# Batch 1's first transform: twelve columns by sums and differences, and a new order in the first block

## The chip, the cores and the metric

The kernel runs on one core of a Trainium2 chip. Its time is the device time of one execution in microseconds; runs of the kernel before took 863.89, 864.54 and 865.01 (median 864.54). One more execution was profiled. Engines are named as the profile names them: PE (TensorE; PEld is its weight load), DVE (VectorE), ACT (ScalarE), POOL (GpSimd) and SP (SyncE, which only issues DMAs here).

## The reference

Two stages follow each other. `x` is 8 batches of 3008 tokens by 256 features in fp32. First, each feature is filtered along the tokens with a real FFT; then a gated feed-forward net runs over all 24064 tokens.

```
X = np.fft.rfft(x, axis=1)
y = np.fft.irfft(X * (filt_r + 1j * filt_i)[None], n=3008, axis=1)
gate = np.maximum(y @ w_gate, 0.0)      # 256 -> 1536
val = y @ w_val                         # 256 -> 1536
out = (gate * val) @ w_out              # 1536 -> 256
```

## The kernel before

**The transform.** The 3008 tokens are seen as 94 rows (n1) by 32 columns (n2). A first product over n1 (the "A" stage) gives 48 frequencies k1, real and imaginary part, for each column. A turn brings columns onto partitions; `fwd` is the product over n2, `product` multiplies with the filter's real part (`tt`, k = 0) and imaginary part (`uu`, k = 1), `inv` goes back over n2, a second turn follows, and `item_c` goes back over n1 and leaves `yT`. `gv` then makes one 128-wide piece of gate and value for 512 tokens: two matmuls into psV, two into psG, a copy of psV by ACT (`vsb`), and one DVE instruction for `prod`. `o_part` multiplies prods with `w_out`.

**Order.** Nothing is scheduled by the framework: each engine runs its instructions in the order of the text. The first block's work is written out by hand: batch 0's A stage, `first_b` (batch 0 from `fwd` to `inv`, with batch 1's A stage put between as `item`s), `turn_d`, the first `item_c`s, and then 47 blocks of 12 `gv`s. Later batches' stages hang on step numbers in `side`. For batches 2 to 7 the A stage works with folded rows: POOL forms sums and differences (`fold_chunk`), and `tiled_a` runs sixteen fp32 matmuls of 24 rows by 32 columns on sixteen tiles of PE. Batches 0 and 1 use one full fp32 matmul for 512 columns instead (`a_bank`).

**Batch 1's A stage** is 16 items: (p, s, h) is columns 8p + 4s to 8p + 4s + 3 and half h of the features. An item is a matmul in `a_bank` and one or two ACT copies (`a_1`). The first half of the features goes to `AS1[0]`, inside dCb, and through DRAM (`store_half`, `load_half`); the rest goes to two `asb` tiles that DVE turns in `turn_1`. Its x comes in 12 DMAs on SP (`load_x`), each to every fourth of 128 partitions, in the order of the columns, behind a small DMA (`hold`) that waits for filter data.

**PSUM banks.** `bank` takes the bank that was given back longest ago (`free.pop(0)`), `done` puts one back. So the order of `done` calls in the text says which earlier reader an instruction waits for.

**Memory.** The prologue's tiles (pool `pro`) hold WA, tabs (with conj and M1's source), the products of batch 0 and more. `prologue.close()` at line 696 frees them, and pool `fs` (vsb, prod, osb and others) takes the same memory.

**POOL's list in this part** is: the six products of `ON_POOL` (it reads a copy `xs` that ACT makes of PSUM), `place_own`, the loads of WvT, WgT (two halves each) and WoT (two halves), the copy of M1, the sign change of Fti (line 694, which reads conj), and later the loads of batch 2's x.

Of the kernel before, what the change touches and what calls it, by code (L numbers as in the profile page):

```python
# [12 lines left out]
FP32 = mybir.dt.float32  # L13
BF16 = mybir.dt.bfloat16
ALU = mybir.AluOpType
# [14 lines left out]
N1, N2 = 94, 32  # L30
# [86 lines left out]
def kernel(  # L117
# [20 lines left out]
    assert NB * W == B * S  # L138

    wa_h, fold_h, f2_h, tab_h = _tables()  # L140

    ctx.enter_context(tc.manual_schedule())
    consts = ctx.enter_context(tc.tile_pool(name="consts", bufs=1))
# [12 lines left out]
    def done(t):  # L156
        free.append(held.pop(id(t))[0])
# [7 lines left out]
    XF = [consts.tile([128, NX2 * D], FP32, name=f"XF{c}") for c in range(N2 // NX2)]  # L165
    XP = [t[:, i * 2048:i * 2048 + 2048].rearrange("p (k d) -> p k d", d=512) for t in XF for i in range(2)]
    WA = pro.tile([128, 128], FP32)
    AS0 = pro.tile([128, 4, N2 // 2, D // 8, 4], BF16)
    DS0 = AS0.rearrange("p q n c f -> p (q n c f)").rearrange("p (k c f) -> p k c f", c=D // 2, f=4)
    dCb = consts.tile([128, 48, D], BF16)  # L170
# [91 lines left out]
    def a_bank(n2, nn, d0, nd):  # L262

        psA = bank("psA", nn, nd)
        xf = XF[n2 // NX2].rearrange("p (n d) -> p n d", d=D)
        n = n2 % NX2
        nc.tensor.matmul(psA, WA, xf[:, n:n + nn, d0:d0 + nd], start=True, stop=True)  # L267
        return psA
# [10 lines left out]
            nc.scalar.copy(dst[:, :, q.start + i], src[:, :, i])  # L279
        done(psA)  # L280

    def a_1(p, s, h):

        psA = a_bank(NC2 * p + 4 * s, 4, h * D // 2, D // 2)
        if h and len(AS1) == 1:
            for _ in range(2):
                t = sb.tile([128, NC2 * D], BF16, tag="asb", bufs=3, name="asb")
                AS1.append(t.rearrange("p (l c d) -> p l c d", l=NC2, c=N2 // NC2))
        ts = AS1[1:] if h else AS1[:1]
        w = D // 2 // len(ts)  # L290
        for i, t in enumerate(ts):
            nc.scalar.copy(t[:, 4 * s:4 * s + 4, p, :], psA[:, :, i * w:(i + 1) * w])
        done(psA)

    def turn_a(dst, src):

# [17 lines left out]
    def new_at(b):  # L314
        shape = [2, 32, D // 2] if b else [16, D // 2, 4]
        ats[b] = sb.tile([128, *shape], BF16, tag="at", bufs=1, name="at")
# [70 lines left out]
            nc.sync.dma_start(ats[b][:, 8 * z:8 * z + 8].rearrange("p j d -> p (j d)"),  # L387
                              _ap(Abuf[b], 8 * z * D, [[NG * D, 128], [1, 8 * D]]))

    ON_POOL = ((0, 1), (1, 1), (2, 1))  # L390
    ats = {}

    psXs, tus, left, xs = {}, {}, {}, {}
# [43 lines left out]
    def inv(b, q):  # L437

        psD = [bank("psD", 2, D) for c in range(4)]
        last = 0 if b else 1  # L440
        for m in range(2):
            for k in range(last + 1):
                for r in range(2):
                    for c in range(4):
                        for e in range(2):
                            i = 2 * q + m
                            nc.tensor.matmul(psD[c][64 * e:64 * e + 64, m],  # L447
                                             (I2t, I2u)[k][32 * c:32 * c + 32, r, 2 * i + e, :],
                                             tus[b, i, e, k][32 * c:32 * c + 32, r],
                                             start=(k == r == 0), stop=(k == last and r == 1),  # L450
                                             tile_position=(32 * c, 64 * e))
        dst = sb.tile([128, 8, D], BF16, tag="dsb", bufs=3, name="dsb") if b else DS0
        def out(cs):
            for c in cs:
                copy = nc.vector.tensor_copy if (c % 2 if b else (q, c) in ((1, 3), (2, 0), (2, 1))) else nc.scalar.copy
                if b:
                    copy(dst[:, c:8:4, :], psD[c])
                else:
                    k, g = 4 * q + c // 2, c % 2 * 2
                    copy(dst[:, k:k + 3:2, :, g:g + 2], psD[c].rearrange("p m (f e) -> p m e f", f=2))  # L460
                done(psD[c])
        if not b:
            return out(range(4))

        def rest():
            out((2, 3))
            for z in range(4):
                nc.sync.dma_start(_ap(Dbuf[b], (64 * (z // 2) + z % 2) * NG * D + 8 * q * D,
                                      [[2 * NG * D, 32], [1, 8 * D]]),
                                  dst[32 * z:32 * z + 32])  # L470
        out((0, 1))
        return rest

    def first_b(item):

        def products(i, es=(1, 0)):
            for e in es:
                for k in range(2):
                    product(0, i, e, k, pool=(i, e) in ON_POOL)

        for i in range(3):
            fwd(0, i)
            if i < 2:
                products(i)
        make_back_u()
        products(2)
        warm(3)
        fwd(0, 3)
        products(3, (1,))
        warm(3)  # L490
        fwd(0, 4)
        item(2)
        products(3, (0,))
        inv(0, 0)
        fwd(0, 5)
        products(4)
        item(2)
        products(5)
        place_own()
        inv(0, 1)  # L500
        item(2)
        inv(0, 2)

    dCs = {}
# [161 lines left out]
            warm(4)  # L666
    hold = sb.tile([2, 8], BF16, tag="hold", bufs=1)
    nc.sync.dma_start(hold, Ftr[0:2, 4, 0:8])
    load_x(1, sp, ((0, 0, 2 * q), (0, 2 * q, 4 * q), (1, 0, 2 * q), (1, 2 * q, 4 * q)))
    items = iter([(p, s, h) for p in range(4) for h in range(2) for s in range(2)])  # L670

    def item(n):
        for _ in range(n):
            p, s, h = next(items)
            a_1(p, s, h)
            if (p, s, h) == (3, 1, 0):
                new_at(1)
                store_half(1)
                load_half(1)

    first_b(item)
    load_vg(0, DFF // 2)
    load_vg(DFF // 2, DFF)
    load_o()
    nc.gpsimd.tensor_copy(M1, tabs[:, 578:].rearrange("p (l n) -> p l n", l=2))
    for h in range(2):
        turn_d(h)
    item(7)
    for m in range(y_items(0)):
        for h in range(2):  # L690
            item_c(m, h)
    item(3)
    turn_1(0)
    nc.gpsimd.tensor_scalar(Fti, Fti, conj[:, 0:1], 1.0, op0=ALU.mult, op1=ALU.mult)
    nc.sync.dma_start(WF, nc.inline_tensor(fold_h, name="dft_fold").ap())
# [89 lines left out]
```

## Time and profile before

| | us |
|---|---|
| median of three runs | 864.54 |
| profiled execution | 863.39 |
| its span | 861.6 |
| PE busy | 853.8 |
| DVE busy | 578.6 |
| ACT busy | 500.2 |
| POOL busy | 458.0 |
| start of the first psX (batch 0's fwd) | 22.33 |
| start of the first psV | 45.85 |
| start of the first psO | 57.49 |

In a timeline a line gives the start and the duration in us, the engine, the source line, the operation, what it writes and reads, its shape and the number of merged instructions; in brackets stands the idle time ahead of it and what ended it. In a table of windows each engine's busy time comes with its number of instructions, followed by PE's granted clock, the DMA engines' mean busy share and GB/s. Matmuls are pipelined, so a duration is longer than the distance to the next start.

### The profile page before, as it was taken

The page shows a single profiled execution, that of the slowest core. Times are in us where ns is not written, and L with a number is a line of the kernel's source. Part 1 is how long each engine was busy: PE and PEld are TensorE (multiplying, and loading weights), DVE is VectorE, ACT ScalarE, POOL GpSimd, SP SyncE. Part 2 cuts the span into 40 slices and gives each one's busy share as a digit, 9 for nine tenths or more (in the row PEclk, how much of TensorE's full clock was granted, in tenths as well). Part 3 has the DMA queues.
Part 4 walks back from the last instruction along what each step waited for, and adds up shares of the span by engine and source line. Part 5 has one row for each costly group of instructions (what it writes and reads, how often), then busy time and mean ns, then how long its engine had stood idle before and what let it go on. Part 6 is the DMA issues. An engine that isn't in the chain of part 4 may idle for free.

```text
span 861.6 us, 20366 instructions
## 1 busy us (share of the span) xinstructions
PE 853.8 (99%) x7614; PEld 497.3 (58%) x7614; DVE 578.6 (67%) x864; ACT 500.2 (58%) x944; POOL 458.0 (53%) x494
## 2 busy tenths in 40 slices
PE   9999999999999999999999999999999999999997
PEld 4456655656556555665556665565655656666665
DVE  3878865777657876577765787658766578555554
ACT  5765565556655565555655565655565555565552
POOL 6747890488986765776667756867550033000001
PEclk9999999999999999999999999999999999999999
DMA  9995375333762339534294333842454222511112
GB/s 248 239 166 124 98 156 145 104 113 106 195 190 79 80 92 190 175 84 102 73 211 153 99 101 94 201 147 77 103 118 119 97 62 51 129 39 31 37 32 55
DMA packets 102862, 101.60 MB, mean 118 GB/s; under 512 B 21703, under 2 KB 89959, under 8 KB 101995
## 3 DMA queue, kind: packets, MB, share of 16 engines
q1 hardware_dynamic: 83407, 77.93, 34.1%
q0 software_dynamic: 18848, 21.68, 11.6%
q8 instruction: 60, 0.98, 0.5%
q10 hardware_dynamic: 508, 0.68, 0.3%
q14 instruction: 39, 0.32, 0.1%
HBM read 58.23 MB, written 45.88 MB: 121 GB/s over the span
## 4 chain that ended last, share of the span: by engine, by line
PE 98%; DMA 1%; SPq 1%; issue 0%; ACT 0%; DVE 0%
PE psV L578 29%; PE psO L599 29%; PE psG L578 28%; PE psF L369 3%; PE psA L267 3%; PE psY L561 3%; PE psD L447 2%; PE psX L404 1%; DMA XF<-in_x_dram 1%; SPq L192 1%; PE psI L209 0%; ACT AS L460 0%; DVE XF L608 0%; SPq L637 0%
## 5 line engine op out<-in xcount | busy, mean ns | idle before, releaser
L583 DVE SCALAR_TENSOR_TENSOR prod<-psG,vsb 128x512 bf16<-128x512 f32 x564 | 389.5, 691 | 234.0 <-ACT vsb L581 229.9
L581 ACT CAST vsb<-psV 128x512 bf16<-128x512 f32 x564 | 332.4, 589 | 217.6 <-PE psV L578 210.2
L599 PE MATMUL psO<-WoT,prod 128*128 128x256 bf16 x2256 | 336.5, 273 | 0.0
L578 PE MATMUL psV<-yT,WvT 128*128 128x512 bf16 x1128 | 336.2, 380 | 0.0
L578 PE MATMUL psG<-yT,WgT 128*128 128x512 bf16 x1128 | 335.3, 379 | 0.0
L599 PEld LDWEIGHTS <-prod 128*128 128x128 bf16 x2256 | 220.7, 98 | 143.4
L578 PEld LDWEIGHTS <-WgT 128*128 128x128 bf16 x1128 | 110.0, 97 | 133.9 <-issue 1.1
L434 POOL TENSOR_TENSOR pp<-tt,uu 128x256 bf16<-128x256 f32 x84 | 61.1, 727 | 169.8 <-DVE uu L424 159.9
L578 PEld LDWEIGHTS <-WvT 128*128 128x128 bf16 x1128 | 100.4, 98 | 36.9 <-issue 25.6
L569 ACT CAST yT<-psY 128x470 bf16<-128x470 f32 (+16 forms) x134 | 58.8, 457 | 46.6 <-PE psY L561 46.5
L608 ACT COPY osb<-psO 128x512 f32<-128x512 f32 x92 | 53.9, 586 | 25.2 <-PE psO L599 24.1
L621 POOL DMA_DIRECT2D out_dram<-osb x5 | 2.6, 539 | 119.2 <-ACT osb L608 117.7
L424 DVE TENSOR_TENSOR tt<-psX,Ftr 128x512 f32<-128x512 f32 (+1 forms) x93 | 63.5, 683 | 0.5 <-PE psX L404 0.5
L424 DVE TENSOR_TENSOR uu<-psX,Fti 128x512 f32<-128x512 f32 (+1 forms) x93 | 63.3, 681 | 0.2 <-DMA Fti<-in_filt_i_dram 0.2
L435 POOL TENSOR_TENSOR pp<-tt,uu 128x256 bf16<-128x256 f32 x84 | 61.0, 726 | 0.0
L355 POOL TENSOR_TENSOR fold<-XF 128x1024 f32<-128x1024 f32 x24 | 56.5, 2352 | 4.8 <-DMA XF<-in_x_dram 4.3
L356 POOL TENSOR_TENSOR XF<-XF 128x1024 f32<-128x1024 f32 x24 | 56.5, 2355 | 1.9
L259 POOL CAST scr<-prod 128x8 f32<-128x8 bf16 x19 | 3.6, 192 | 85.7 <-DVE prod L583 85.7
L342 POOL DMA_DIRECT2D XF<-in_x_dram x76 | 45.7, 604 | 2.1 <-issue 1.0
L376 DVE CAST asb<-psF 128x512 bf16<-128x512 f32 x48 | 30.9, 686 | 17.7 <-PE psF L369 17.7
L376 ACT CAST asb<-psF 128x512 bf16<-128x512 f32 x48 | 25.8, 589 | 28.9 <-PE psF L369 28.9
L561 PE MATMUL psY<-M,dCb 96*128 96x94 bf16 (+2 forms) x514 | 39.9, 205 | 0.0
(68 smaller groups left out, 456.4 us busy)
## 6 DMA issues: line engine op xcount, KB each, us to landing
Dbuf<-dsb SPq DMA_DIRECT2D x84, 128.0 KB
dCb<-Dbuf SPq DMA_DIRECT2D x56, 192.0 KB
XF<-in_x_dram POOLq DMA_DIRECT2D x38, 256.0 KB, 7.4
Abuf<-asb SPq DMA_DIRECT2D x96, 96.0 KB
at<-Abuf SPq DMA_DIRECT2D x18, 512.0 KB
XF<-in_x_dram SPq DMA_DIRECT2D x31, 256.0 KB
XF<-in_x_dram POOLq DMA_DIRECT2D x76, 96.0 KB, 5.2
out_dram<-osb SPq DMA_DIRECT2D x69, 94.0 KB
```

The costliest lines, as they stand in the source:

```text
L355: tt(t, xp[:, 0:2], xp[:, 2:4], op=ALU.add)
L356: tt(xp[:, 2:4], xp[:, 0:2], xp[:, 2:4], op=ALU.subtract)
L376: copy(asf[:, :, q, :], banks[q])
L424: nc.vector.tensor_tensor(p, psX, filt, op=ALU.mult)
L434: nc.gpsimd.tensor_tensor(p[:, 0], tt[:, 0], uu[:, 1], op=ALU.subtract)
L435: nc.gpsimd.tensor_tensor(p[:, 1], tt[:, 1], uu[:, 0], op=ALU.add)
L561: nc.tensor.matmul(psY[:, o:o + w], d_rows(b, col, h), M1[:, 1, n1:n1 + w] if b == 0 else M1[:NROW, 0, n1:n1 + w], start=True, stop=True)
L569: copy(yT[:, h, p:p + w], psY[:, o:o + w])
L578: nc.tensor.matmul(pt[:, :W], w[:, h, ft * 128:(ft + 1) * 128], yT[:, h, y0:y0 + W], start=(h == 0), stop=(h == 1))
L581: nc.scalar.copy(vsb, psV[:, :W])
L583: nc.vector.scalar_tensor_tensor(prod, in0=psG[:, :W], scalar=0.0, in1=vsb, op0=ALU.max, op1=ALU.mult)
L599: nc.tensor.matmul(psO[:, t % 2], prods[ft][:, t * 128:(t + 1) * 128], WoT[:, ft, :], start=(ft == 0), stop=(ft == NFT - 1))
```

## The change

`WH` holds the rows of WA's table for n1 = 0 to 46, once at partitions 0 and once at 64. Since row n1 + 47 has the same coefficient as row n1 up to a sign that is + for even k1 and - for odd ones, sums of the two rows give the even frequencies and differences the odd ones.

- `load_halves` loads nn columns so that partition n1 has rows n1 and n1 + 47 side by side, the first half of the columns at partitions 0 to 47 and the second at 64 to 111. `fold_halves` makes sums and differences on POOL. `a_halves` runs four fp32 matmuls of 47 rows by 64 columns on four tiles, into two banks, and `out_1` copies a bank to the places that `a_1` filled.
- Columns 8 to 15 (two `a_halves`, one for each half of the features) and 28 to 31 (one, with all features) go that way; items are left for p = 0, p = 2 and the first half of p = 3: ten.
- `first_b` has five items, one fewer ahead of `inv(0, 2)`. Its first products are ordered otherwise: on POOL tt, tt, uu, uu of two groups and later the third, on DVE three tt and then three uu. One more copy of `inv(0, 1)` goes to DVE.
- On POOL, `fold_halves(8, 8)`, M1 and `fold_halves(28, 4)` stand between the first and the second half of the weights WvT and WgT. On SP, 14 DMAs replace 12.
- `store_half` and `load_half` follow the last `a_halves`, behind the `item_c`s.

```diff
+    wh_h = np.zeros_like(wa_h)
+    n1 = np.arange(N1 // 2)
+    for r in (0, 64):
+        wh_h[r + n1] = wa_h[n1 % 32 * 4 + n1 // 32]
...
+    WH = pro.tile([128, 128], FP32)
...
-    def a_1(p, s, h):
-
-        psA = a_bank(NC2 * p + 4 * s, 4, h * D // 2, D // 2)
-        if h and len(AS1) == 1:
+    def out_1(psA, n2, n, d0, nd):
+
+        if len(AS1) == 1:
...
-        ts = AS1[1:] if h else AS1[:1]
-        w = D // 2 // len(ts)
-        for i, t in enumerate(ts):
-            nc.scalar.copy(t[:, 4 * s:4 * s + 4, p, :], psA[:, :, i * w:(i + 1) * w])
+        l, p = n2 % NC2, n2 // NC2
+        for t, lo, w in zip(AS1, (0, D // 2, 3 * D // 4), (D // 2, D // 4, D // 4)):
+            if d0 <= lo < d0 + nd:
+                nc.scalar.copy(t[:, l:l + n, p, :], psA[:, :, lo - d0:lo - d0 + w])
         done(psA)
+
+    def a_1(p, s, h):
+
+        n2, d0 = NC2 * p + 4 * s, h * D // 2
+        out_1(a_bank(n2, 4, d0, D // 2), n2, 4, d0, D // 2)
+
+    def halves(n2, nn):
+
+        o = n2 % NX2 * D
+        return XF[n2 // NX2][:, o:o + nn * D].rearrange("p (k n d) -> p k n d", k=2, d=D)
+
+    def load_halves(b, n2, nn):
+
+        w = nn // 2
+        for s in range(2):
+            nc.sync.dma_start(halves(n2, nn)[64 * s:64 * s + 48].rearrange("p k n d -> p k (n d)"),
+                              _ap(x, (b * N1 * N2 + n2 + w * s) * D,
+                                  [[N2 * D, 48], [N1 // 2 * N2 * D, 2], [1, w * D]]))
+
+    sums = {}
+
+    def fold_halves(n2, nn):
+
+        xh = halves(n2, nn)
+        sums[n2] = pro.tile([128, nn // 2, D], FP32, tag=f"sum{nn}", name="sum")
+        nc.gpsimd.tensor_tensor(sums[n2], xh[:, 0], xh[:, 1], op=ALU.add)
+        nc.gpsimd.tensor_tensor(xh[:, 1], xh[:, 0], xh[:, 1], op=ALU.subtract)
+
+    def a_halves(n2, nn, d0, nd):
+
+        w, d = nn // 2, slice(d0, d0 + nd)
+        banks = [bank("psA", w, nd) for _ in range(2)]
+        for e, src in ((1, sums[n2]), (0, halves(n2, nn)[:, 1])):
+            for s in range(2):
+                r = 64 * s
+                nc.tensor.matmul(banks[s][64 * e:64 * e + 64], WH[r:r + N1 // 2, 64 * e:64 * e + 64],
+                                 src[r:r + N1 // 2, :, d], start=True, stop=True, tile_position=(r, 64 * e))
+        for s in range(2):
+            out_1(banks[s], n2 + w * s, w, d0, nd)
...
-                copy = nc.vector.tensor_copy if (c % 2 if b else (q, c) in ((1, 3), (2, 0), (2, 1))) else nc.scalar.copy
+                copy = nc.vector.tensor_copy if (c % 2 if b else (q, c) in ((1, 2), (1, 3), (2, 0), (2, 1))) else nc.scalar.copy
...
         for i in range(3):
             fwd(0, i)
-            if i < 2:
-                products(i)
+        for k in range(2):
+            for i in range(2):
+                product(0, i, 1, k, pool=True)
+        for i in range(3):
+            product(0, i, 0, 0)
         make_back_u()
-        products(2)
+        for k in range(2):
+            product(0, 2, 1, k, pool=True)
+        for i in range(3):
+            product(0, i, 0, 1)
...
-        item(2)
+        item(1)
         inv(0, 2)
...
-    load_x(1, sp, ((0, 0, 2 * q), (0, 2 * q, 4 * q), (1, 0, 2 * q), (1, 2 * q, 4 * q)))
-    items = iter([(p, s, h) for p in range(4) for h in range(2) for s in range(2)])
+    load_x(1, sp, ((0, 0, 2 * q),))
+    load_halves(1, 8, 8)
+    nc.sync.dma_start(WH, nc.inline_tensor(wh_h, name="dft_wh").ap())
+    load_x(1, sp, ((1, 0, 2 * q), (1, 2 * q, 3 * q)))
+    load_halves(1, 28, 4)
+    items = iter([(p, s, h) for p in (0, 2, 3) for h in range(2) for s in range(2 - p // 3)])
...
-            if (p, s, h) == (3, 1, 0):
-                new_at(1)
-                store_half(1)
-                load_half(1)
...
     load_vg(0, DFF // 2)
+    fold_halves(8, 8)
+    nc.gpsimd.tensor_copy(M1, tabs[:, 578:].rearrange("p (l n) -> p l n", l=2))
+    fold_halves(28, 4)
     load_vg(DFF // 2, DFF)
     load_o()
-    nc.gpsimd.tensor_copy(M1, tabs[:, 578:].rearrange("p (l n) -> p l n", l=2))
     for h in range(2):
         turn_d(h)
-    item(7)
+    item(3)
+    for h in range(2):
+        a_halves(8, 8, h * D // 2, D // 2)
+    item(2)
     for m in range(y_items(0)):
         for h in range(2):
             item_c(m, h)
-    item(3)
+    a_halves(28, 4, 0, D)
+    new_at(1)
+    store_half(1)
+    load_half(1)
     turn_1(0)
```

More of the change, by code (lines that the diff above doesn't have):

```diff
@@ L388, in load_at_tiled @@
                               _ap(Abuf[b], 8 * z * D, [[NG * D, 128], [1, 8 * D]]))
-    ON_POOL = ((0, 1), (1, 1), (2, 1))
     ats = {}
@@ L478, in products @@
                 for k in range(2):
-                    product(0, i, e, k, pool=(i, e) in ON_POOL)
+                    product(0, i, e, k)
         for i in range(3):
             fwd(0, i)
-            if i < 2:
-                products(i)
+        for k in range(2):
[3 more added lines that the diff above has]
+            product(0, i, 0, 0)
         make_back_u()
-        products(2)
+        for k in range(2):
+            product(0, 2, 1, k, pool=True)
+        for i in range(3):
+            product(0, i, 0, 1)
         warm(3)
@@ L668 @@
     nc.sync.dma_start(hold, Ftr[0:2, 4, 0:8])
-    load_x(1, sp, ((0, 0, 2 * q), (0, 2 * q, 4 * q), (1, 0, 2 * q), (1, 2 * q, 4 * q)))
-    items = iter([(p, s, h) for p in range(4) for h in range(2) for s in range(2)])
+    load_x(1, sp, ((0, 0, 2 * q),))
[4 more added lines that the diff above has]
+    items = iter([(p, s, h) for p in (0, 2, 3) for h in range(2) for s in range(2 - p // 3)])
     def item(n):
         for _ in range(n):
-            p, s, h = next(items)
-            a_1(p, s, h)
-            if (p, s, h) == (3, 1, 0):
-                new_at(1)
-                store_half(1)
-                load_half(1)
+            a_1(*next(items))
     first_b(item)
     load_vg(0, DFF // 2)
+    fold_halves(8, 8)
+    nc.gpsimd.tensor_copy(M1, tabs[:, 578:].rearrange("p (l n) -> p l n", l=2))
+    fold_halves(28, 4)
     load_vg(DFF // 2, DFF)
     load_o()
-    nc.gpsimd.tensor_copy(M1, tabs[:, 578:].rearrange("p (l n) -> p l n", l=2))
     for h in range(2):
         turn_d(h)
-    item(7)
+    item(3)
+    for h in range(2):
+        a_halves(8, 8, h * D // 2, D // 2)
+    item(2)
     for m in range(y_items(0)):
```

## The prediction

> **What bounds the kernel now.** I read the page's chain first, then the waits of TensorE after the prologue (there are none after 57 us), then the timelines of TensorE, POOL, ACT and DVE between 20 and 55 us. Below are two lines of the page and seven of TensorE's timeline (start, duration).
>
> ```profile
> PE   853.8 (99%) x7614; PEld 497.3 (58%) x7614; DVE 578.6 (67%) x864; ACT 500.2 (58%) x944; POOL 458.0 (53%) x494
> ...
> PE 98%; DMA 1%; SPq 1%; issue 0%; ACT 0%; DVE 0%
> ...
> 26.93 1.96 PE L267 MATMUL psA<-XF,WA 128*128 128x512 f32 x4 [0.68 <-DMA XF<-in_x_dram]
> ...
> 35.39 0.42 PE L447 MATMUL psD<-tt,I2t 32*64 32x256 bf16 x16
> ...
> 36.40 6.28 PE L267 MATMUL psA<-XF,WA 128*128 128x512 f32 x14
> 42.66 0.70 PE L561 MATMUL psY<-M,dCb 128*128 128x94 bf16 x12
> 43.20 2.81 PE L267 MATMUL psA<-XF,WA 128*128 128x512 f32 x6
> 45.85 0.59 PE L578 MATMUL psV<-yT,WvT 128*128 128x512 bf16 x2
> ...
> 111.61 1.14 PE L369 MATMUL psF<-XF,WF 24*32 24x512 f32 x32
> ```
>
> TensorE never stops from the first psV (45.85) to the end, so whatever moves the first block's matmuls moves the end by as much. The change works ahead of 45.85. There an item (one fp32 matmul, two records) costs 6.28/7, about 0.86 to 0.9 us. The psF line is sixteen fp32 calls on sixteen small tiles in 1.08 us (111.61 to the next psV at 112.69): two passes of 0.43 and 0.22 for going in and out.
>
> Three other engines meet TensorE there; these are their timelines:
>
> ```profile
> 36.38 2.82 POOL L694 TENSOR_SCALAR Fti<-Fti,tabs 128x3072 bf16<-128x3072 bf16 x1
> ...
> 37.89 4.72 DVE L302 STREAM_TRANSPOSE dCb<-AS 128x2048 f32<-128x2048 f32 x2
> ...
> 46.61 1.32 ACT L581 CAST vsb<-psV 128x512 bf16<-128x512 f32 x2
> ...
> 46.45 1.09 DVE L297 STREAM_TRANSPOSE at<-asb 128x512 f32<-128x512 f32 x1 [2.32 <-ACT asb L292]
> 47.44 1.24 DVE L583 SCALAR_TENSOR_TENSOR prod<-psG,vsb 128x512 bf16<-128x512 f32 x2
> 48.60 1.08 DVE L297 STREAM_TRANSPOSE at<-asb 128x512 f32<-128x512 f32 x1
> 49.58 1.84 DVE L583 SCALAR_TENSOR_TENSOR prod<-psG,vsb 128x512 bf16<-128x512 f32 x3
> ```
>
> POOL is done with the prologue at 39.20 and idle to 53. The first vsb copy writes memory of the closed pool pro, and among its waits is POOL's count at L694, the last use of that pool; today that is 7 us old. DVE runs behind TensorE in the first gv steps: the third prod ends at 50.23.
>
> **The change on TensorE's path.** *Products.* DVE no longer waits 0.2 us for Fti; its 18 products end at 33.66, not 33.96. Nothing waits for that, so it is worth 0. But banks are handed out in the order they were given back. With the new order fwd(0,4) gets the bank of (2,1), which ACT empties into xs from 26.12 to 26.68. fwd(0,4) starts at 26.75, not 25.82, and the item behind it, which waited for its load until 26.93, starts at 27.08 (16 matmuls and the switch are 0.33, from 36.07 to 36.40): 0.15 lost. POOL's six products only change places.
>
> *Last inverse sooner.* One item fewer ahead of it: 35.39 + 0.15 - 0.86 = 34.68. Its operands are ready at 33.66. DVE takes two copies of inverse 1 and two of inverse 2; as in the trace the latter start 1.10 after the inverse, so the transposes start 0.7 sooner and end at 41.9.
>
> *Tiled columns.* inv(0,2) takes 1.01 (35.69); then five items (4.31), two a_halves and the switches. For two in a row I take four passes and one 0.22, 1.95, from the psF row; a third alone 1.08. That gives psY at 42.15, with the transposes hidden (41.9). If nothing overlapped between the four tiles, an a_halves would be 4 x 0.86 = 3.45; psF, the nearest row, says otherwise. psY 0.54, the third a_halves 1.08: first psV at 43.8, where yT, on DVE 1.47 after psY's start as now, is ready at 43.6. TensorE alone gains 2.05.
>
> *Loads on SP.* Fourteen DMAs for twelve, with the same bytes and 64 KB for WH. The two first halves loads put 786 KB on 48 neighbouring partitions each, not on every fourth. Rows of the table of windows:
>
> ```profile
> 28.00:30.00 2.00, 2.00 (x83) 1.00 (x81) 2.00 (x4) 1.26 (x3) 2.00 (x3) 1.00 0.86 328
> 30.00:32.00 2.00, 1.69 (x20) 0.68 (x4) 2.00 (x4) 2.00 (x5) 1.94 (x4) 1.00 1.02 402
> ...
> 46.00:48.00 2.00, 2.00 (x11) 0.88 (x9) 1.55 (x2) 1.74 (x4) 0.00 (x0) 1.00 0.82 164
> 48.00:50.00 2.00, 2.00 (x11) 0.93 (x10) 2.00 (x4) 1.24 (x3) 0.00 (x0) 1.00 0.68 191
> ```
>
> (The last column is GB/s.) Strided loads run at 254 to 402, the store from 24 neighbouring partitions at 164 to 191. 786 KB is 2.0 to 3.1 us or 4.1 to 4.8 us; I take 2 us more, as the store is nearest in shape. The ninth load landed at 31.76; the item ahead of inv(0,2) would get it at 33.8 where it wants it at 33.6: 0.2 at most, covered below. The halves land near 31.2, and those of 28 to 31 near 36.5. [...]
>
> **The change on POOL, which I think decides.** Today, after place_own: two weight DMAs to 32.93, then the rest. Now the folds come in: 2 x 2.35 (as L355/L356, same shape) to 37.65, M1 0.34, two of 128x512 at 1.27 to 40.5. The other four weight DMAs take 3.08 as now (43.6), Fti 2.82: end at 46.5 instead of 39.2. The sums are ready 0.7 before the first a_halves (38.4), those of 28 to 31 two us before theirs. But the first vsb waits for 46.5. ACT would be ready for it at 45.1: the third a_halves leaves it six small copies, 1.2 us by an estimate from its 0.65 for two of 256 columns, and cover for them is gone with POOL's wait anyway. So vsb starts at 46.55, practically when it does now (46.61), and DVE follows it: first prod at 47.2 (now 47.44, where a transpose held it), second 47.8, turn_1(1) 48.4, third 49.4 to 50.05. There are eight banks. The fifth psG needs the first prod's, the seventh psV (now at 51.24) the third prod's, since a psY takes one bank between. So the seventh psV cannot start before 50.1: 1.15 sooner, not 2.05. After that DVE gains 0.26 a step and TensorE is not held again: prod 4 is done at 51.25, wanted at 51.6. The gain is the smaller of the two, 1.15; I round down to 1.1 for waits that POOL takes between DMAs. Up to 0.9 of lateness in TensorE's own part (the loads, the tiles, the 0.15) is hidden by this.
>
> *Weights.* These lines are from the answers for the two tiles. The second halves of WvT and WgT are issued at 40.55 and 41.25, not 32.93 and 33.64, and are wanted at 50.1 and 50.5.
>
> ```profile
> L247 POOL DMA_DIRECT2D WvT<-in_moe_w_val_dram x2: 716/754/793, 31.4 to 32.9; - x2
> ...
> DMA to landing us min/median/max: 6.7/8.6/10.6
> ...
> L247 POOL DMA_DIRECT2D WgT<-in_moe_w_gate_dram x2: 716/722/728, 32.2 to 33.6; - x2
> ...
> DMA to landing us min/median/max: 7.8/9.5/11.2
> ```
>
> The short ones are the first pair, behind x; the long ones queued behind the first pair. With 6.7 and 7.8 they land at 47.3 and 49.1: no stall. With 10.6 and 11.2, at 51.2 and 52.5: 2.0 lost. I take the short ones, as the first pair is long gone by then. The store of batch 1's half (issued near 44.8, now 44.94) meets them, though. WoT, wanted at 56.4, and fwd(1,0), wanted at 59.5 with its half landing at 56.5 now, have 2 to 3 us each.
>
> **Sum.** The profiled execution took 863.39 (span 861.6 and 1.8 around it); the median of the three runs is 864.54, 1.15 above. 864.54 - 1.1 = 863.4. About 0.2% (1.73 us) is what a measurement of this kernel can tell from no change, so my forecast lies inside that.
>
> **Rivals.**
> 1. *The whole gain arrives.* If vsb need not wait for L694, or POOL is done by 45, TensorE's 2.05 stands: 862.5, faster by 0.24%. For it: no stall of this kind is in the trace of before. Against: the order of the wait and POOL's four durations, all from rows. 0.2.
> 2. *The second weights come late* (the slower side). The seventh gv needs WgT's second half; each us after 50.5 costs one, from 51.6 the kernel is slower than before, from 53.4 by more than 0.2%. With the long landings 864.54 - 1.1 + 2.0 = 865.4; if the store (4.1 to 4.8 us at its rate) goes first, WgT lands at 49.1 + 4.5 = 53.6 and the time is 866.5. For it: DMA share is over 1 from 34 to 46 now. Against: the short landings. 0.14.
> 3. *Four tiles don't overlap as sixteen do.* If only second passes queue (1.3 more for each of three), psV starts at 47.7 and the time is 866.4; psF speaks against it. 0.06.
> 4. *The halves land after 32.93*, so POOL's string starts late. It takes 1.7 us more than I count; with 1.1 more there is no gain: 864.5. 0.06.
> My forecast has 0.54.
>
> **How the numbers follow.** Faster: rival 1 and a bit of a TensorE tail, 0.21. Slower: about half of rival 2, rival 3 and 0.02 for what I don't see, 0.15. The rest, 0.64, is within 0.2%. The range goes from rival 1 with the runs' own spread (0.4), 862.1, to rivals 2 and 3 at their middle, 866.2.
>
> **What would show it.** Right: L694 ends near 46.5 and the first vsb starts just behind it; the first psV is near 43.8, the seventh near 50.1, with idle time of TensorE ahead of the fifth psG and the seventh psV put down to DVE prod; an a_halves pair takes about 1.95; fwd(0,4) waits for ACT xs. Wrong: vsb ahead of L694's end, or TensorE idle at the seventh gv put down to a DMA, or 3 us for an a_halves.

## The result, and the profile after

The changed kernel took 869.5 us in the median of 22 runs (866.08 to 871.6), the kernel before 864.11 in 22 runs on the same chip: a ratio of 1.0054 with a 95% interval of 1.0045 to 1.0064. It is slower by half a per cent, where I had forecast 863.4 and at most 866.2. The profiled execution took 870.49 (span 868.7, against 861.6 before: 7.1 more). Ratios and intervals leave out slow runs (more than 1.5% above the fastest of their kernel), which are three of the ten of the kernel without the gate of Fti below, its profiled one among them, while its median is that of all ten.

PE's busy time and the chain that ended last, from the page of the changed kernel:

```profile
PE 854.0 (98%) x7626; PEld 496.7 (57%) x7626; DVE 578.1 (67%) x865; ACT 499.4 (57%) x946; POOL 465.2 (54%) x498
...
PE 93%; DMA 5%; ACT 1%; SPq 1%; issue 0%; DVE 0%; ACTq 0%
```

PE is as busy as before (853.8), so its idle time is 7 us longer, and DMAs have gone from 1% of the chain to 5%. (Busy time hides two terms that cancel here: what the tiles save, and the 1.7 us that a lower clock costs further down.) PE's four longest waits from 20 to 72 us (line and tile, what it waited for, us, times, longest) say where:

```profile
PE psX L446 <- DMA at<-Abuf: 3.7, 1, 3.7
PE psV L626 <- ACT vsb L629: 1.9, 1, 1.9
PE psX L446 <- ACT xs L463: 0.9, 1, 0.9
PE psV L626 <- DVE prod L631: 0.5, 1, 0.5
```

The largest is not one I had priced: `fwd(1,0)` waits for the half of batch 1 that goes through DRAM. The chain in order of time (start, us, what) shows how it got there, and PE's timeline what happened behind it:

```profile
45.75 0.88 SPq L369
...
46.67 6.75 DMA Abuf<-dCb
...
53.48 0.92 SPq L375
...
54.49 11.40 DMA at<-Abuf
...
66.02 0.63 PE psX L446 x31
```

```profile
66.02 0.63 PE L446 MATMUL psX<-at,F 64*32 64x256 bf16 x31 [3.73 <-DMA at<-Abuf]
66.58 0.82 PE L626 MATMUL psV<-yT,WvT 128*128 128x512 bf16 x2
67.19 1.06 PE L626 MATMUL psG<-yT,WgT 128*128 128x512 bf16 x2
68.05 1.06 PE L647 MATMUL psO<-WoT,prod 128*128 128x256 bf16 x4
68.90 1.06 PE L626 MATMUL psV<-yT,WvT 128*128 128x512 bf16 x2
```

Line 369 is `store_half`, line 375 `load_half`. Their issues on SP, in the kernel before (lines 326 and 332) and then in the changed one:

```profile
44.94 2.69 SPq L326 DMA_DIRECT2D Abuf<-dCb  x4
49.60 2.40 SPq L332 DMA_DIRECT2D at<-Abuf  x4
```

```profile
45.39 2.24 SPq L369 DMA_DIRECT2D Abuf<-dCb  x4
52.03 5.71 SPq L375 DMA_DIRECT2D at<-Abuf  x4
```

The last part of the load took 11.4 us from its issue to its landing (5.1 before, by the same semaphore events), and a pair of psG matmuls that took 0.59 us up to 61 takes 1.06 behind the wait: the table of windows gives a granted clock of 0.71 from 66 to 68, 0.50 from 68 to 70 and 0.94 from 70 to 72.

Counting in starts of `vsb` (564 in each kernel, the same work), the changed kernel is behind the kernel before by

| up to `gv` | behind by, us | what came in |
|---|---|---|
| 6 | 1.39 | the gate of the first vsb, less what PE gained ahead of it |
| 14 | 1.39 | |
| 18 | 7.08 | the wait of 4.0 at `fwd(1,0)`, and 1.7 at the reduced clock |
| 200 | 7.08 | |
| 210 | 7.61 | a wait of ACT on Abuf at 353 us |
| 563 | 7.61 | |

and the end comes 0.5 us sooner behind the last vsb, which leaves the 7.1. So nothing goes wrong after 72 us but that one half microsecond.

### The profile page after: what moved, and what is told of

The parts are those of the page before. It is cut to its first block, busy times and chain, and to the rows that moved or that the text cites. A ratio compares the mean times of both kernels' runs of the same rounds, so it can differ in the third digit from the quotient of the medians.

```text
span 868.7 us, 20400 instructions
## 1 busy us (share of the span) xinstructions
PE 854.0 (98%) x7626; PEld 496.7 (57%) x7626; DVE 578.1 (67%) x865; ACT 499.4 (57%) x946; POOL 465.2 (54%) x498
## 4 chain that ended last, share of the span: by engine, by line
PE 93%; DMA 5%; ACT 1%; SPq 1%; issue 0%; DVE 0%; ACTq 0%
PE psO L647 28%; PE psV L626 27%; PE psG L626 27%; PE psY L609 3%; PE psF L412 3%; PE psA L272 2%; PE psD L489 2%; DMA Abuf<-asb 1%; PE psX L446 1%; DMA at<-Abuf 1%; DMA dCb<-Dbuf 1%; DMA Abuf<-dCb 1%; DMA XF<-in_x_dram 1%; SPq L197 0%; PE psA L333 0%; ACT I2u L225 0%
## 5 line engine op out<-in xcount | busy, mean ns | idle before, releaser
L398 POOL TENSOR_TENSOR fold<-XF 128x1024 f32<-128x1024 f32 x24 | 56.4, 2351 | 7.2 <-DMA XF<-in_x_dram 6.7
L399 POOL TENSOR_TENSOR XF<-XF 128x1024 f32<-128x1024 f32 x24 | 56.5, 2354 | 1.9
L385 POOL DMA_DIRECT2D XF<-in_x_dram x76 | 45.6, 602 | 4.6 <-DMA XF<-in_x_dram 2.1
```

What stands on the lines that cost most here:

```text
L398: tt(t, xp[:, 0:2], xp[:, 2:4], op=ALU.add)
L399: tt(xp[:, 2:4], xp[:, 0:2], xp[:, 2:4], op=ALU.subtract)
```

## The experiments

Each kernel ran beside the kernel before on the same chip. This table is worked out from the profiled executions: first psV less first psX is PE's way through the first block, "held" is the time from the store's first issue to its first packet, "load" the time from `load_half`'s first issue to its last landing, and the wait is PE's at `fwd(1,0)` for Abuf.

| kernel | median us | ratio to before, interval | psV - psX | held | load | wait |
|---|---|---|---|---|---|---|
| before | 863.9 to 865.5 | 1 | 23.5 | 0.8 | 6.9 | 0 |
| after | 869.5 | 1.0054, 1.0045 to 1.0064 | 21.7 | 5.0 | 13.9 | 3.7 |
| gate of Fti gone | 872.81 | 1.0058, 1.0022 to 1.0095 | 22.8 | 4.3 | 21.6 | 13.2 |
| weights first | 864.34 | 1.0006, 0.9990 to 1.0022 | 23.8 | 0.8 | 8.5 | 0 |
| 28 to 31 sooner | 866.82 | 1.0025, 1.0008 to 1.0043 | 22.9 | 3.6 | 10.6 | 2.4 |
| before, late weights (first try) | 869.66 | 1.0065, 1.0047 to 1.0083 | 29.5 | 3.7 | 7.1 | 0 |
| before, late weights | 875.33 | 1.0132, 1.0096 to 1.0168 | 23.1 | 4.5 | 15.6 | 4.7 |
| after, batch 2's x later | 874.25 | 1.0103, 1.0084 to 1.0122 | 23.9 | 3.4 | 9.8 | 0.3 |
| before, new products | 865.13 | 1.0011, 0.9991 to 1.0032 | 26.1 | 0.8 | 7.4 | 0 |
| early, old products | 862.59 | 0.9980, 0.9967 to 0.9993 | 23.4 | 0.8 | 8.4 | 0 |
| early, new products | 862.26 | 0.9975, 0.9962 to 0.9988 | 23.8 | 0.8 | 7.6 | 0 |
| split sums | 862.66 | 0.9977, 0.9964 to 0.9989 | 23.6 | 0.8 | 8.9 | 0 |
| split sums, old products | 862.81 | 0.9970, 0.9951 to 0.9990 | 24.6 | 0.8 | 8.5 | 0 |
| split sums, more warm | 862.36 | 0.9961, 0.9948 to 0.9974 | 22.9 | 0.9 | 7.9 | 0 |

### Is it the gate of Fti?

The changed kernel, with Fti's sign taken from a tile of the pool that stays, so that vsb's memory has no reader on POOL any more.

```diff
-    conj32 = pro.tile([128, 2], FP32, tag="conj32", bufs=1)
+    conj32 = consts.tile([128, 2], FP32, name="conj32")
...
-    nc.gpsimd.tensor_scalar(Fti, Fti, conj[:, 0:1], 1.0, op0=ALU.mult, op1=ALU.mult)
+    nc.gpsimd.tensor_scalar(Fti, Fti, conj32[:, 0:1], 1.0, op0=ALU.mult, op1=ALU.mult)
```

> The changed kernel with conj32 kept outside the prologue's pool, so that the sign change of Fti is no longer a last use of that pool. Theory 1 (two waits in a row: first the vsb copies behind Fti, then fwd(1,0) behind batch 1's half, which the second weights hold up in the DMA queues): the first vsb starts near 45.7 instead of 49.1, the seventh psV near 50 to 51 instead of 52.6, but the half lands when it did (65 to 66), so fwd(1,0) only waits longer (5 to 6 us instead of 3.7) and the time stays within 1 us of the changed kernel's. Rival (the vsb wait is what costs the time): 2 to 3 us faster than the changed kernel, 866.5 to 867.5.

The gate is gone: the first vsb starts at 46.1 and not at 49.1, and `gv` 6 is 1.06 us ahead of the kernel before, not 1.39 behind. The time is no better: PE comes sooner to a half that is not there sooner. The ten runs lie between 864.4 and 879.8, wider than those of the changed kernel, and their median is 3.3 above its median, not within 1. The profiled execution is one of the longest three (878.14) and doesn't stand for the median: its half landed at 73.8 and PE waited 13.2 us for it, where I had expected 65 to 66 and 5 to 6. Why its load ran for 21.6 us no run here shows. The gate was real, but a larger wait stood behind it.

### Is it the late weights?

POOL issues the second weights and WoT ten microseconds later than before; its timeline in the kernel before and then in the changed one:

```profile
32.93 0.72 POOL L247 DMA_DIRECT2D WvT<-in_moe_w_val_dram  x1
33.64 0.72 POOL L247 DMA_DIRECT2D WgT<-in_moe_w_gate_dram  x1
34.35 1.66 POOL L253 DMA_DIRECT2D WoT<-in_moe_w_out_dram  x2
```

```profile
43.10 0.74 POOL L252 DMA_DIRECT2D WvT<-in_moe_w_val_dram  x1
43.83 0.72 POOL L252 DMA_DIRECT2D WgT<-in_moe_w_gate_dram  x1
44.54 1.66 POOL L258 DMA_DIRECT2D WoT<-in_moe_w_out_dram  x2
```

First, the changed kernel with all six weight transfers ahead of the sums:

```diff
     load_vg(0, DFF // 2)
+    load_vg(DFF // 2, DFF)
+    load_o()
     fold_halves(8, 8)
...
     fold_halves(28, 4)
-    load_vg(DFF // 2, DFF)
-    load_o()
```

> The changed kernel with all six weight DMAs issued ahead of the folds on POOL, as before the change. Theory 1: the weights land by 46 again, the store's first packets leave within 1 us of its issue, the half lands near 56.5 and fwd(1,0) waits for nothing; the differences for columns 8 to 15 are ready at 40.8 instead of 37.9, so TensorE waits some 2 us ahead of them; Fti ends near 46.5 to 47; time 863.5 to 865. Rival (the half is late because its store stands later, behind the last A stage matmuls, whatever POOL does): the half still lands at 62 to 66 and the time stays at 868 to 870.

That takes away nearly the whole loss: 864.34, the same as before within the interval. The store's first packet leaves 0.8 us after the issue, the half lands at 59.4, and PE has no wait from 44 to 72 us. POOL's sums start 3.6 us later for it, and PE waits 0.6 us for them.

Then the other way round: the kernel before with only the second weights late. The first try put 9.6 us of idle sums ahead of them:

> The kernel before, with 9.6 us of sums on POOL that nobody reads between the first and the second half of the weights, so that the second halves and WoT are issued near 42.5 as in the changed kernel; conj32 outside the pool, so that no vsb waits for Fti. Nothing else of the change is in it. Theory 1: the store, issued near 44.9, sends its first packets only near 50, the half lands at 62 to 66 where fwd(1,0) wants it at 60.6, TensorE waits 3 to 5 us and runs at a lower granted clock after that; time 868 to 871. Rival (the lateness comes from the new loads, folds and the later store): same as before, 864 to 864.6.

This one can't be read as meant. The copy of M1 stood behind the sums on POOL, psY waited for it (1.9 us in the list of waits), two stretches of 3.4 us at a granted clock of 0.50, from 27.1 and from 47.5, cost about 3.4 more, psV was 6 us late, and PE came to `fwd(1,0)` at 66.6, behind the half. It does show that the store is held (3.7 us). The second try copies M1 first (and has conj32 in the pool that stays, as the first had):

```diff
     load_vg(0, DFF // 2)
+    nc.gpsimd.tensor_copy(M1, tabs[:, 578:].rearrange("p (l n) -> p l n", l=2))
+    idle = pro.tile([128, 1024], FP32, tag="idle", bufs=1)
+    for w in (1024, 1024, 1024, 512, 512):
+        nc.gpsimd.tensor_tensor(idle[:, 0:w], XF[0][:, 0:w], XF[0][:, 1024:1024 + w], op=ALU.add)
     load_vg(DFF // 2, DFF)
     load_o()
-    nc.gpsimd.tensor_copy(M1, tabs[:, 578:].rearrange("p (l n) -> p l n", l=2))
```

> The kernel before, its data path whole, with 9.6 us of sums on POOL that nobody reads (1024, 1024, 1024, 512 and 512 fp32 columns of XF) between the first weights and the second weights and WoT; M1 is copied ahead of them this time, and Fti's sign is read from a tile of the pool that stays, so that neither M1 nor Fti can hold psY or vsb. Left over is one thing: the second weights and WoT are issued at about 43.5 to 46.5 us, as in the changed kernel, and not at 33 to 36. Theory 1 (weights in flight hold the store of batch 1's half): the store is issued near 45 us, its first packet leaves at 49 to 51 (before: 0.8 us after the issue), load_half's four parts land at 57 to 66, fwd(1,0), wanted at 60.6, waits 2 to 5 us, the clock falls after it, and the time is 867 to 871. Rival 2 (the half is late in the changed kernel because of its own order on PE, ACT and SP, and late weights alone cost nothing): first packet within 1.5 us of the issue, landings by 57, 863.8 to 864.8.

PE's two longest waits from 20 to 75 us in it:

```profile
PE psX L404 <- DMA at<-Abuf: 4.7, 1, 4.7
PE psG L578 <- DMA WgT<-in_moe_w_gate_dram: 1.5, 1, 1.5
```

Up to `gv` 6 it is level with the kernel before to 0.01 us; at `gv` 8 it is 1.66 behind (WgT, which landed at 53.3, 9.0 us after its issue), at `gv` 18 9.35 behind. Without a single folded column, late weights alone cost more than the whole change does: theory 1 holds, and the time lies even above its range (871.8 to 880.2 in six runs).

### Does the half meet batch 2's x as well?

The hold explains a store 4 us late. In the changed kernel the load itself also took 13.9 us, not 6.9. From 56 us on POOL issues the first loads of batch 2's x, so I moved those:

```diff
-            loads, folds = (((6, 12, 20, 30), (22, 34, 46, 46)) if b == 2 else
+            loads, folds = (((20, 24, 28, 32), (36, 42, 46, 50)) if b == 2 else
```

> The changed kernel with the four loads of batch 2's x at steps 20, 24, 28, 32 in place of 6, 12, 20, 30 (their folds at 36, 42, 46, 50 in place of 22, 34, 46, 46). Nothing else moves: the second weights and WoT still leave POOL at 43 to 46 us, and the store should still be held to about 50 us. In the changed kernel the last part of the half landed at 65.9 us, 14 us after load_half's first issue, where before it took 8 to 9. Theory 1 (two causes in a row: the store is held 4 to 5 us by the weights, and then the half's load runs beside batch 2's x on the same 16 engines, which costs it 4 to 6 us more): the half lands at 59 to 62.5, fwd(1,0) at 62.0 waits under 0.7 us, the clock stays at 1.00, and the time is 864 to 866. Rival 2 (the held store alone is enough; x costs the load nothing): the half lands at 64 to 66, the wait is 2.5 us or more, 868 to 870.5. Rival 3 (the moved loads collide with batch 1's way back or the folds and cost there): no wait at fwd(1,0), a new one between 70 and 110 us, over 866.

Of PE's waits from 44 to 72 us the one at `fwd(1,0)`, and then the longest from 72 to 120:

```profile
PE psX L446 <- DMA at<-Abuf: 0.3, 1, 0.3
```

```profile
PE psD L489 <- POOL pp L476: 5.2, 2, 4.2
```

The store is still held (3.4 us), but the load takes 9.8 us, its last part 7.6 from issue to landing in place of 11.4, and the wait at `fwd(1,0)` shrinks from 3.7 to 0.3 (2.5 of it because the half lands sooner, 0.9 because PE, which had lost its clock at 28 us in this execution, came later). The first try above agrees: its load ran behind WoT's last packet (55.4) and, up to 61.4, ahead of x's first, and took 7.1. So theory 1 is right on the mechanism: two causes stand in a row. On the total, rival 3 is right: batch 2's folds (9.8 us each on POOL) now stand between POOL's additions for batch 1, PE waits 5.2 us for those, its clock reads 0.50 from 116.7 to 123.5, behind the longer of the two waits, and the time is 874.25.

### Are the loads of columns 28 to 31 late?

On POOL, the changed kernel stood idle 2.35 us ahead of the sums for columns 28 to 31. POOL's timeline (start, us, line, operation, idle time ahead in brackets):

```profile
37.83 0.34 POOL L731 COPY M<-tabs 128x188 bf16<-128x188 bf16 x1
40.51 1.29 POOL L323 TENSOR_TENSOR sum<-XF 128x512 f32<-128x512 f32 x1 [2.35 <-PE psA L333]
```

PE had nothing to do with it: POOL sat in a wait for DMA semaphores up to 40.4, and the two loads landed at 39.6 and 40.4. They had been issued at 32.2 and 32.5, behind a wait of SP's for earlier landings. So I put them ahead of the load for columns 24 to 27:

```diff
-    load_x(1, sp, ((1, 0, 2 * q), (1, 2 * q, 3 * q)))
+    load_x(1, sp, ((1, 0, 2 * q),))
     load_halves(1, 28, 4)
+    load_x(1, sp, ((1, 2 * q, 3 * q),))
```

> The changed kernel with the two loads for columns 28 to 31 issued ahead of those for 24 to 27. Theory 1 with the late landing as a cause of its own (the loads were issued at 32.2 behind the landing of the loads for 8 to 15, and met the first weights): they land near 33 instead of 40.4, POOL's fold of them starts at 38.2 instead of 40.5, Fti ends near 46.6, the first vsb starts there, the second weights are issued near 40.8 instead of 43.1, the half lands 2 to 3 us sooner and fwd(1,0) waits 0 to 2 us; time 865 to 867. Rival (landing makes no difference, the wait at 38.2 was for TensorE's matmuls on columns 8 to 15): POOL still starts at 40.5 and the time is that of the changed kernel.

The loads land at 36.0 and 36.6 (near 33 expected), the sums start at 38.06, Fti ends at 46.60 instead of 49.07 (46.5 in the prediction), the first vsb starts at 46.77, and `gv` 6 is 0.4 ahead of the kernel before. The weights leave POOL 2.5 us sooner, too, so the half lands at 62.8, and the wait is 2.4 (0 to 2 expected). Half of the loss is gone; what is left is the same wait.

### The order of the first products, and the clock

Alone on the kernel before:

```diff
-            if i < 2:
-                products(i)
+        for k in range(2):
+            for i in range(2):
+                product(0, i, 1, k, pool=True)
+        for i in range(3):
+            product(0, i, 0, 0)
         make_back_u()
-        products(2)
+        for k in range(2):
+            product(0, 2, 1, k, pool=True)
+        for i in range(3):
+            product(0, i, 0, 1)
```

> The kernel before with the order of the first products alone (three tt, then three uu; all three pairs of POOL copied from xs first). Theory 1: fwd(0,4) waits about 0.9 us for ACT's xs as in the changed kernel, inv(0,2) is not sooner by itself, so the path to psY is 0.1 to 0.4 us longer: 864.1 to 864.6. Rival 2: the order itself moves the POOL weights and the items of batch 1 and costs more than a microsecond: over 865.2. Rival 3: it gains, because the three first products end sooner: under 863.7.

`fwd(0,4)` starts at 26.74 with a wait for xs of 0.7, as in the changed kernel (26.82). The twelve runs go from 863.6 to 869.8, and the interval holds no change as well as 0.3%; it is not settled whether the order alone costs anything. The profiled execution shows what can happen to it, in PE's table of windows (busy, instructions, granted clock, DMA share, GB/s):

```profile
26.00:28.00 2.00, 0.43 (x17) 1.00 0.93 283
28.00:30.00 2.00, 1.96 (x3) 0.55 0.89 291
30.00:32.00 2.00, 2.00 (x34) 0.60 0.92 311
```

PE idled most of 26 to 28, the clock fell, and the passes of the items behind started 0.85 us apart, where 0.43 is usual. This execution is 2.67 us behind before at `gv` 0 and stays there.

The version with split sums (below) lost its clock in the same place, so I gave it the old order, and separately more junk to run (`warm`, matmuls whose result nobody reads):

```diff
-        warm(3)
+        warm(4)
         fwd(0, 3)
         products(3, (1,))
-        warm(3)
+        warm(6)
```

> The version with split sums, with the old order of the first products. In the profile with the new order PE stood idle 1.4 of the 4 us from 24 to 28, and the granted clock read 0.59, 0.50, 0.50 and 0.70 in the four microseconds from 27 to 31, while in the kernel before it read 1.00 there. Theory 1 (the new order's longer wait ahead of fwd(0,4) is what tips the clock, in most executions): no drop from 26 to 32, 0.8 to 1.6 us faster than the split sums with the new order, 861.0 to 861.9. Rival 2 (the drop comes with PE's idle time there whatever the order of products): the drop stays, 862.3 to 863. Rival 3 (the clock doesn't drop, but the order of the first products was itself worth the same): 862.2 to 862.8 at a clock of 1.00.

> The version with split sums and the new order of products, with 4 and 6 products of junk in place of 3 and 3 ahead of fwd(0,3) and fwd(0,4) (one is 0.21 us at the full clock): they lie in PE's waits there. Theory 1 (PE's idle time tips the clock): no drop from 26 to 32, 861.0 to 862.0. Rival 2 (the drop has another cause, or the junk runs into the fwd behind it): the drop stays or fwd(0,4) is 0.4 us later, 862.4 to 863.2.

PE's windows in the old order, and then with more junk:

```profile
26.00:28.00 2.00, 1.33 (x5) 0.92 0.97 324
28.00:30.00 2.00, 1.93 (x18) 0.50 0.94 248
```

```profile
26.00:28.00 2.00, 2.00 (x25) 1.00 0.86 291
28.00:30.00 2.00, 2.00 (x31) 1.00 0.94 234
```

The old order keeps the drop (862.81: rival 2), the junk removes it (862.36, and twelve runs within 861.98 to 862.81, the narrowest of all). So it isn't the order; that PE's idle time there tips the clock is likely, by one profiled execution of each, but idle time isn't all of it: the version with early weights and the old products (below) idled for 2.2 of the 4 us from 24 to 28 and kept 1.00. 862.36 also lies above theory 1's 861.0 to 862.0. The median gains only 0.3 us on the split sums (on another chip), under the 1 us that I had set for a drop in most executions: how often it comes wasn't measured.

### What is left of the four tiles

With the causes known, the change can be put together otherwise: all six weight transfers ahead of the sums, columns 28 to 31 loaded ahead of 24 to 27, five whole items ahead of the two `a_halves` calls, conj32 in the pool that stays. Once with the old order of products and once with the new:

```diff
     load_x(1, sp, ((0, 0, 2 * q),))
+    load_x(1, sp, ((1, 0, 2 * q),))
     load_halves(1, 8, 8)
+    load_halves(1, 28, 4)
     nc.sync.dma_start(WH, nc.inline_tensor(wh_h, name="dft_wh").ap())
-    load_x(1, sp, ((1, 0, 2 * q), (1, 2 * q, 3 * q)))
-    load_halves(1, 28, 4)
+    load_x(1, sp, ((1, 2 * q, 3 * q),))
...
-    item(3)
+    item(5)
     for h in range(2):
         a_halves(8, 8, h * D // 2, D // 2)
-    item(2)
```

> The changed kernel with the order of the first products as before, all six weight transfers issued ahead of the sums, the loads for columns 28 to 31 ahead of those for 24 to 27, the five whole items ahead of the two calls of a_halves for columns 8 to 15, and Fti's sign from a tile that stays. Theory 1 (the loss is the late weights, the gate of Fti and the late sums; the four tiles themselves save about 1.5 us on PE): first psV at 44 to 44.8 us, store packets within 1.2 us of the issue, load_half landed by 58, no wait at fwd(1,0), 862.2 to 863.4. Rival 2 (the halves of 48 partitions and the sums cost as much elsewhere, so nothing is left of the tiles): 863.8 to 864.8. Rival 3 (the store is held by something else than the weights): fwd(1,0) still waits 2 us or more, 866 to 870.

> The same as the run with the early weights and the old order of products, but with the new order (three tt, then three uu). Theory 1: 0.1 to 0.4 us over that run, 862.4 to 863.8; the difference is fwd(0,4)'s wait for ACT. Rival 2: the new order lets inv(0,2) and so the sums start sooner, and it is faster than that run by 0.2 us or more. Rival 3: fwd(1,0) still waits 2 us or more, 866 to 870.

Both beat the kernel before, by 0.20% and 0.25%; the two intervals overlap, so which order of products is better stays open. The first psV is no sooner (45.6 and 45.95): theory 1's time came out with the old order (with the new one 862.26 is 0.1 below its range), its path on PE didn't. Up to `gv` 200 the profiled executions are 0.25 ahead of the kernel before (old order) and 0.1 behind (new), and the end comes 0.5 sooner behind the last vsb, for a reason that no run here shows; so it isn't shown that the gain of 1.4 to 1.7 us in the medians is the tiles'. In the run with the new order the last item waited 1.2 us for columns 24 to 27, and the sums weren't ready before 41.2. So the next version loads 24 to 27 ahead of 28 to 31 and makes the sums of columns 8 to 15 in two halves of the features:

```diff
+        nd = D // cuts
+        for d in (slice(c * nd, c * nd + nd) for c in range(cuts)):
+            nc.gpsimd.tensor_tensor(sums[n2][:, :, d], xh[:, 0, :, d], xh[:, 1, :, d], op=ALU.add)
+            nc.gpsimd.tensor_tensor(xh[:, 1, :, d], xh[:, 0, :, d], xh[:, 1, :, d], op=ALU.subtract)
```

> The early-weights version with the new products, in which PE waited 1.2 us for columns 24 to 27 at 38.3 us and then, in effect, for the sums of columns 8 to 15 until 41.4: now columns 24 to 27 are loaded ahead of 28 to 31, and the sums and differences of columns 8 to 15 are made in two halves of 128 channels, each sum followed by its difference. Theory 1 (the sums bound that stretch): first a_halves near 39.6, psY at 42.1 to 42.6 (DVE's turn_d ends at 42.0 and is the next bound), first psV near 44.2 to 44.8, 860.6 to 861.8. Rival 2 (ACT, which copies 20 tiles between 38 and 47 us, is the bound and takes the gain back): psY sooner but vsb at 46.5 or later, 861.9 to 862.6. Rival 3 (smaller sums hold DVE's copies and the order of the loads delays the third item): no gain or a loss, 862.3 to 863.5.

862.66: no better, and not theory 1's 860.6 to 861.8. The waits for XF are gone from PE's list, but the clock fell to 0.50 from 28 to 30 in the profiled execution, psY came at 43.7, and vsb at 46.74. With the junk that drop is gone: psY at 42.7, the first psV 22.9 us after the first psX (23.6 with split sums, 23.5 before), and a ratio of 0.9961 (0.9948 to 0.9974), the lowest of all, though its interval overlaps those of the other early versions and its median (862.36) isn't the lowest. Its profiled span is 860.65, 0.97 below before's: 0.46 at the `gv`s and 0.5 at the end. The medians differ by 3 us because the kernel before was slower beside it, with 865.33, than beside the first two early versions (863.94). The two fastest runs differ by 1.1.

## Why the prediction was wrong

**The step that failed** is the last sentence on the weights: "WoT, wanted at 56.4, and fwd(1,0), wanted at 59.5 with its half landing at 56.5 now, have 2 to 3 us each." I had seen that the store meets the late weights, and gave that no price for the store, only for WgT (rival 2). The last part of the half landed 9.4 us later, at 65.9, and PE wanted it at 62.0. Two terms make the 9.4. `load_half` was issued 2.4 us later than before: the store was issued 0.5 later and its first packet waited 5.0 us and not 0.8, of which its faster passage gave 2.2 back (its 8 KB packets took 322 ns in the median, 572 before). And the load ran for 13.9 us and not 6.9: with batch 2's x moved it took 4.1 less, with the weights moved 5.4 less, which is no sum, since each of the two also shifts what the other meets.

The hold can't be read from the trace of before, where the store's first packet left 0.8 us after its issue. In all six runs with the weights late no packet left for 3.4 to 5.0 us, against 0.8 or 0.9 in the others. The trace's packets show what differs: when the store was issued, 1406 to 2048 packets of the second weights and WoT had yet to start in the six, and 40 to 524 in the other eight. The DMA engines were busy in both (a share of 0.96 to 1.18 in the microseconds from 45 to 50, the hold of the changed kernel, and 1.46 from 44 to 46 before). How a backlog on POOL's queue holds a store on SP's no run here shows.

**What it cost beyond the wait.** I had no term for the clock. Behind 4 us of idle time it was 0.50 from 66.8 to 70.3 (0.71 and 0.50 in the two windows given above), which cost 1.7. With columns 28 to 31 sooner a wait of 2.4 us brought the same drop, from 63.9 to 67.3, and the same loss. At 24 to 28 idle time alone doesn't tell the runs apart: PE was busy for 2.6 of these 4 us with split sums and lost its clock, and for 1.8 with early weights and the old products and kept it. The clock records of the changed kernel begin at 5.40, 66.84, 70.25 and 868.97 us: 18, 1 and 234 times 3.413 us apart. The two of the kernel before, at 4.96 and 861.71, are 251 times that apart. Counted in stretches of 3.41 us from an execution's own steps, PE was busy for 0.8 us of the stretch ahead of the drop at 66.8, and for 1.0 of the one ahead of the drop at 63.9. Such a count doesn't tell all runs apart either: one with 2.0 us was followed by a drop (split sums, up to 27.2), ones with 1.9 (early weights and the old products, up to 25.9) and 1.5 (changed kernel, 46.4 to 49.8) were not. What makes the clock fall no run here shows.

**Step by step.**
- *Products*: right. `fwd(0,4)` waited 0.86 for xs and the item behind started at 27.17 (27.08 forecast).
- *Last inverse*: 35.10, not 34.68; the item ahead of it came at 34.08.
- *Tiled columns*: right. Two `a_halves` take 1.87 (38.89 to 40.76; 1.95 forecast), the third 1.04 (1.08), so rival 3 falls. First psV at 44.22, 1.63 sooner than before for the 2.05 forecast; the 0.42 between them is the last inverse's.
- *Loads on SP*: the halves of 8 to 15 landed at 30.4 and 32.1 (near 31.2 forecast), those of 28 to 31 at 40.4 and not at 36.5. This put 2.35 us of idle time into POOL, which I had not counted. Rival 4 looked at the wrong pair of loads.
- *The gate*: the mechanism was right, the size off. ACT's timeline:

```profile
49.11 2.05 ACT L629 CAST vsb<-psV 128x512 bf16<-128x512 f32 x4 [3.40 <-POOL Fti L749]
```

Fti ended at 49.07, not 46.5 (2.35 of it POOL's idle time), so vsb was 2.5 later than before and not level with it. PE was held at the fifth psV (1.9) and the seventh (0.5). In place of a gain of 1.15 there was a loss of 1.39 (0.24 of it a later first psX). Rival 1 falls with the wait; without the gate `gv` 6 is 1.06 ahead, but 0.3 of it is an earlier first psX, so 0.75 is left of the 2.05 that rival 1 gave such a kernel (in that execution PE also waited 1.3 for XF near 27 us, 0.7 before).
- *Weights*: WvT and WgT landed 5.1 and 7.0 us after their issue, under the short durations that I took, and PE didn't wait for them (0.3 each for WgT and WoT in the execution without the gate). WoT's second half landed at 58.4, 0.5 us ahead of the first psO, so its 2 to 3 us of slack were gone too. Rival 2 had the right cause (weights and store in each other's way) and the wrong victim.

In sum: -1.1 forecast; +1.39 at the gate, +4.0 at `fwd(1,0)`, +1.7 for the clock, +0.5 at 353 us and -0.5 at the end measured, 7.1 together.

## What to carry to other kernels

A step moved on one engine's queue moves the transfers it issues, and these must be priced against every transfer that will then be in flight, not only against their own readers: here the victim was a store from another queue whose data PE wanted 17 us later. Work out slack as landing time under the new traffic, not as today's landing time against today's need. And a wait of PE can cost more than its length: here 1.7 us more, behind waits of 2.4 and of 3.7, because the clock then read 0.50 for 3.4 us.

## What the runs showed of the hardware

- A store issued on SP sent no packet for 3.4 to 5.0 us in six kernels in which POOL had issued weight loads in the 7 us before it (in one, WoT just behind it) and 1406 packets of them or more had yet to start; in the eight in which the last of those loads was issued 9.8 us or more ahead of it and 524 packets or fewer were left, it started in 0.8 or 0.9.
- 256-byte packets of `load_half`: its four parts took 6.9 us in all before, and 13.9 beside WoT and batch 2's x. With x moved they took 9.8.
- A granted clock that had fallen stayed at 0.50 for 3.41 us in the changed kernel (66.84 to 70.25) and for about 7 in the second kernel with late weights (0.54 from 66 to 68, 0.50 from 68 to 72; its mean clock of 0.996 over 871.1 us gives 7.0). The steps in the traces of the changed kernel and the kernel before are whole multiples of 3.413 us apart (18, 1 and 234; 251). In the first block the clock fell in five profiled executions near 27 to 28 us, each time behind a stretch in which PE idled for part of 24 to 28 us (for 1.4 us with split sums, 2.2 with the products alone); the execution with the products alone was 2.7 us behind with it, its wait included. Early weights with the old products idled there for 2.2 us and kept 1.00. In the one profile with more junk, four matmuls or about 0.85 us of it, it stayed at 1.00.
- In the kernels that fold columns 8 to 15 and 28 to 31 the end comes 0.5 us sooner behind the last vsb than in the others. SP's last waits for semaphores end sooner (9.0 us behind the start of the last vsb, not 9.6); why, no run here shows.
